# A decode step over two attention and MLP layers: ring of 3808 columns, three slots for the MLP weights of round one, two VectorE instructions fewer per head

## The chip, the cores and the metric

The kernel runs on one core of one Trainium2 chip. The metric is the device time of one execution in microseconds (us). The kernel before has a median of 712.35 us over three runs (711.5 to 712.86).

All data are float32. A column below means one float32 in each of 128 partitions, so 512 bytes; 512 columns are 0.262 MB.

## The reference, cut to what matters

Four sequences, one new token each, model width 640. A layer A (32 heads of width 128, the last 1024 positions of a cache) and a layer B (an MLP of width 1728 with relu) are applied twice, with the same weights and the same caches both times:

```
W = 1024; k = k_cache[:, :, -W:, :]; v = v_cache[:, :, -W:, :]      # B = 4, H = 32, Dh = 128

def A(x):
    q = (x @ wq) split into 32 heads
    p = softmax(einsum("bhqd,bhkd->bhqk", q, k) * Dh ** -0.5)
    return concat(einsum("bhqk,bhkd->bhqd", p, v)) @ wo

def B(x):
    return maximum(x @ w1, 0) @ w2

x = x + A(layernorm(x)); x = x + B(layernorm(x))      # round one
x = x + A(layernorm(x)); x = x + B(layernorm(x))      # round two
```

The four sequences have caches of their own, so each head needs its own 4 x 1024 keys and values, and each of them is used for one query only.

## The kernel before, in words

**Data in memory.** Each head has one record `rec` of `REC` = 9472 columns: 640 of wq (`WQ` to `K`), 4096 of keys (`K` to `V`), 4096 of values (`V` to `WO`), 640 of wo. Keys and values each come in two halves of `VH` = 2048 columns. The MLP weights `wm` are 17,280 columns: w1 as five blocks k of 1728, then w2 as 54 tiles of 160 (`W2` is the column where w2 begins, `WM` the end).

**Buffers in SBUF.** `store` holds five records (`NS` = 5) and, ahead of them, `FIRST` columns; `kept` holds the end of one record; `ring` has `RING` columns. The sum of `FIRST` and `RING` is the same before and after the change. In round one head 0 lies at the start of `store`, and its first `FIRST` columns stay there, so that round two need not load them again; the last five heads of round one (27 to 31) stay too, and round two begins with them (`order`). During the MLP of round one the five records therefore occupy `store`, and the weights pass through `ring` and through `spare`, 2560 columns (`PARKED`) in the middle of head 31's record. The data that lay there are moved to PSUM by four `park` copies (ScalarE) and brought back by `unpark` in round two.

**Order of the loads.** All loads are one list (`items`), issued in that order by SP (SyncE) on its one queue. `MLP_RING` cuts the weights of round one into pieces (from, to, buffer, column); after them `IN_RING` loads that part of head 0's record which isn't resident into `ring` and `spare`; after those, the heads 1 to 5 of round two go, in pieces, to places in the order in which they come free (`places`). A piece is issued when TensorE (PE) has read what stood in its place. So the places are slots: a piece that reuses the place of an earlier one waits until that one has landed, been multiplied and been released.

**One head.** `query` computes q; `scores` multiplies q with the keys, 128 columns of PSUM partitions being four groups of 32, one per sequence, of which only four rows were written; `softmax` is a maximum on VectorE (DVE) and an exponential on ScalarE (ACT), which also gives each partition's sum `tot`; `weights` transposes in 32x32 blocks and scales; `values`, `picks`, `output_T` and `project` finish the head. `scores` of the next head stands ahead of `values` of this one. In `weights` each of the four written rows of a group knows its own sum, and a transpose (`spread`) hands the sum to the other partitions.

**The MLP.** `mlp(0)` goes through w1 block by block (`h_ps`), then relu on DVE, then through w2 tile by tile (`acc`), in groups `W2_RING` after each of which `done` releases a piece. `busy` are matmuls whose result nobody reads; in `mlp(0)` one stands where a piece ends.

In the profile nearly every instruction has line L102, the line of the helper that records it, so groups are told apart by their tiles.

Of the kernel before, what the change touches and what calls it, by code (L numbers as in the profile page):

```python
# [34 lines left out]
OP = mybir.AluOpType  # L35
# [3 lines left out]
P = 128  # L39
B, D, H, DH, W, FF = 4, 640, 32, 128, 1024, 1728  # L40
# [6 lines left out]
WQ, K, V, WO = 0, D, D + 4 * W, D + 8 * W  # L47
REC = 2 * D + 8 * W
# [7 lines left out]
ENDS = 28  # L56
TILES[ENDS:ENDS] = [(13, 0), (13, 1)]
TCOLS = len(TILES) * FD
RING = 4320
KEPT = WO - 4 * 512  # L60
FIRST = K + 3 * 512
PARKED = 2560
FROM = V - 1024
W2 = KB * FF
WM = W2 + TCOLS


W2_RING = [8, 5, 16, 10, 11, 4]
MLP_RING = [(0, 1728, "ring", 0), (1728, 3456, "ring", 1728), (3456, 4320, "ring", 3456), (4320, 6480, "spare", 0),
            (6480, 8208, "ring", 0), (8208, W2 + 1280, "ring", 1728), (W2 + 1280, W2 + 2080, "ring", 3456),  # L70
            (W2 + 2080, W2 + 4640, "spare", 0), (W2 + 4640, W2 + 6240, "ring", 0), (W2 + 6240, W2 + 8000, "ring", 1600),
            (W2 + 8000, WM, "ring", 3456)]

IN_RING = [(2176, 4736, "spare", 0), (4736, 6272, "ring", 0), (6272, 8832, "ring", 1536)]

CUTS = [*range(0, K, DH), *range(K, WO, 512), *range(WO, REC + 1, FD)]
W1_SLOT = [[0, 1], [2, 3], [4]]
# [32 lines left out]
def decode_kernel(ctx: ExitStack, tc: tile.TileContext, xf, rec, wm, out):  # L110
    nc = tc.nc
    pe, dve, act, pool, sp = (InOrder(tc, e) for e in (nc.tensor, nc.vector, nc.scalar, nc.gpsimd, nc.sync))
# [5 lines left out]
    wT = scratch[:, :128].rearrange("p (i c j) -> p i c j", i=2, c=16)  # L118
# [4 lines left out]
    spread = scratch[:, 256:288]  # L123
    hT = scratch.rearrange("p (m j) -> p m j", j=32)
    oTs = sb.tile([P, LATE, B], F32, name="oTs")
    qT = sb.tile([P, B], F32, name="qT")
    of_batch = sb.tile([P, B], F32, name="of_batch")
# [3 lines left out]
    mrt = sb.tile([P, B], F32, name="mrt")  # L131
    small = sb.tile([P, 14], F32, name="small")
    nmax, rtot, rstd, eps, eps_dh, ones, unused, sums, tot0, tot1 = (small[:, i:i + 1] for i in range(10))
    squares = small[:, 10:]
    tot = [tot0, tot1]
    store = sb.tile([P, FIRST + NS * REC], F32, name="store")
    kept = sb.tile([P, REC - KEPT], F32, name="kept")
    ring = sb.tile([P, RING], F32, name="ring")

    sc_ps = [ps.tile([P, W], F32, name=f"sc_ps{i}") for i in range(2)]  # L140
# [39 lines left out]
    def home(h, r):  # L180

        if r:
            return FIRST + (h if h >= LAST else h - 6 + LAST) % NS * REC
        return (0 if h < NS else FIRST) + h % NS * REC

    items = []

    at = {("rec", 1, LAST - 1): [(KEPT, REC, "kept", 0)], ("rec", 1, 0): [(0, FIRST, "store", 0)]}
    live = []
    spare = home(H - 1, 0)  # L190
# [49 lines left out]
    ending(0, hs, True)  # L240
    for lo, hi, buf, col in MLP_RING:
        weight(0, lo, hi, buf, col)
# [3 lines left out]
    old = [home(h, 0) for h in hs[:NS]]  # L246
    new = hs[NS:]


    for lo, hi, buf, col in IN_RING:  # L250
        piece(1, new[0], lo, hi, *place(buf, col))
    places = [("store", old[i] + lo, old[j] + hi) for i, lo, j, hi in (
        (0, 0, 0, K), (0, K + 1024, 0, K + VH), (0, K + VH + 1536, 0, V), (1, 0, 1, K), (1, K, 1, K + VH), (1, K + VH, 1, V),
        (0, V, 0, WO), (2, 0, 2, V), (1, V, 1, REC), (3, 0, 3, V), (2, V, 2, REC), (3, V, 4, FROM))]
    places += [("store", 0, FIRST), ("store", old[4] + FROM, old[4] + REC), ("ring", 0, RING)]
    cuts = [h * REC + x for h in new[1:6] for x in CUTS]
    c, end = new[1] * REC, new[6] * REC
    for buf, lo, hi in places:
        if lo == old[1]:
            piece(1, new[0], WO, REC, buf, lo)  # L260
        elif c < end:
            cut = max(x for x in cuts if x <= min(end, c + hi - lo))
            run(1, c, cut, buf, lo)
            c = cut
# [36 lines left out]
    def done(key, lo, hi):  # L301
# [3 lines left out]
        if key == ("rec", 0, 0):  # L305
            lo = max(lo, FIRST)
        for x, y, buf, col in pieces(key):
# [91 lines left out]
    def scores(r, h, s, first=False):  # L399
        key = ("rec", r, h)  # L400
        for i in range(2):
            for b in range(B):
                pe.matmul(sc_ps[s][32 * b:32 * b + 4, 512 * i:512 * i + 512], qT[:, b:b + 1].to_broadcast([P, 4]),
                          cols(key, K + 512 * (B * i + b), 512), start=True, stop=True)
            done(key, K + VH * i, K + VH * i + VH)
            if first and i == 0:
                if r:
                    unpark(0)
                deviation(eps_dh, float(DH), True)
                act.activation(unused, eps, AF.Exp)  # L410
                if r:
                    unpark(1)
# [8 lines left out]

    def weights(s, parts=((0, 2),)):
        if parts[0][0] == 0:

            dve.transpose(spread, tot[s].to_broadcast([P, 32]))
            dve.reciprocal(rtot, spread[:, 0:1])
            dve.tensor_scalar(mrt, of_batch, rtot, None, op0=OP.mult)
        for i, j in parts:
            w = sc_ps[s][:, 512 * i:512 * j]
            dve.transpose(w, w)  # L430
            dve.tensor_tensor(wT[:, i:j].rearrange("p i c j -> p (i c) j"),
                              w.rearrange("p (c j) -> p c j", j=32)[:, :, :B],
                              mrt.unsqueeze(1).to_broadcast([P, 16 * (j - i), B]), op=OP.mult)

    def values(r, h, last=False, fill=(0, 0)):
        key = ("rec", r, h)
# [25 lines left out]
    def mlp(r):  # L462
# [21 lines left out]
        key = ("w", r)  # L484
        sizes = W2_SLOT if r else W2_RING
        first = 0
# [15 lines left out]
    for r in range(2):  # L502
# [12 lines left out]
        for n, h in enumerate(hs[:-2]):  # L515
            i = n - (H - late)
            s = (n + 1) % 2
# [87 lines left out]
```

## Time and profile before

| | |
|---|---|
| median of three runs | 712.35 us |
| profiled execution | 712.79 us, of which the span of instructions is 711.0 us |
| mean granted TensorE clock | 0.813 |
| busy: PE, DVE, ACT | 501.7 us (71%), 317.6 us (45%), 99.6 us (14%) |
| SP's load queue | 12528 packets, 301.42 MB, 98.9% of 16 engines' span |
| end of the loads | from 707 to 708 us the DMA engines are 1% busy; the store of the result follows |

How to read it: the share of the DMA engines and the moved GB/s by stretch tell where loads set the pace. PE's busy share is high because its clock is low in many stretches: in slices of 10 us it is granted between 0.50 and 1.00.

### The profile page before, as it was taken

Reading aid. Unit: us, or ns where it says so; the run is one execution under the profiler, and the core shown is the slowest. Engines: PE = TensorE matmul, PEld = TensorE weight load, DVE = VectorE, ACT = ScalarE, POOL = GpSimd, SP = SyncE. Lnnn points to the kernel's source line nnn. Section 1 sums busy time; section 2 is a strip of 40 time slices with the busy share of each in tenths; the row PEclk is TensorE's granted clock in tenths of the full one; section 3 lists DMA queues with packets and bytes.
Section 4 is the critical chain, followed back from the end, with each engine's and each line's share of the span. In section 5 each row is a group of like instructions: output and inputs, shape, how many; then the busy total and the mean of one; then the engine's idle time right before and its main releaser. Section 6 shows DMA issues by size and latency. Waiting matters only on the chain.

```text
span 711.0 us, 8606 instructions
## 1 busy us (share of the span) xinstructions
PE 501.7 (71%) x3722; PEld 203.5 (29%) x3722; DVE 317.6 (45%) x646; ACT 99.6 (14%) x210; POOL 1.1 (0%) x9
## 2 busy tenths in 40 slices
PE   0775684678584578869888999655584678686986
PEld 0331231232231223323223343222231232233322
DVE  3252362353353353545631876525162353454751
ACT  0110110011010110111120422101010011011120
POOL 0000000000000000000000000000000000000000
PEclk9987797677778776887999999859597677777999
DMA  9999999999999999999999999999999999999996
GB/s 397 435 417 450 425 431 443 421 439 439 424 435 441 427 436 419 424 438 426 429 398 403 402 427 436 442 438 436 435 420 444 431 435 430 429 433 419 429 427 281
DMA packets 12597, 301.97 MB, mean 425 GB/s; under 512 B 1408, under 2 KB 1552, under 8 KB 4624
## 3 DMA queue, kind: packets, MB, share of 16 engines
q1 hardware_dynamic: 12528, 301.42, 98.9%
q8 instruction: 29, 0.48, 0.2%
q14 instruction: 8, 0.07, 0.0%
q10 hardware_dynamic: 32, 0.01, 0.0%
HBM read 301.34 MB, written 0.08 MB: 424 GB/s over the span
## 4 chain that ended last, share of the span: by engine, by line
DMA 72%; PE 22%; DVE 4%; issue 1%; ACT 1%; ACTq 0%; SPq 0%; DVEq 0%
DMA store<-rec 65%; PE sc_ps L102 8%; PE o_ps L102 6%; DMA store<-wm 5%; PE acc L102 4%; PE misc L102 3%; DMA ring<-wm 2%; DVE scratch L102 1%; PE t_ps L102 1%; DVE o_ps L102 1%; ACT oTs L102 1%; DVE small L102 0%; DVE sc_ps L102 0%; ACT sc_ps L102 0%; ACTq L102 0%
## 5 line engine op out<-in xcount | busy, mean ns | idle before, releaser
L102 PE MATMUL sc_ps<-store,qT 128*4 128x512 f32 x1024 | 186.6, 821 | 42.4 <-DMA store<-rec 41.0
L102 PE MATMUL misc<-xT,store 128*128 128x4 f32 x620 | 95.7, 281 | 112.5 <-DMA store<-rec 112.5
L102 PE MATMUL o_ps<-store,scratch 128*16 128x512 f32 x960 | 145.8, 688 | 2.9 <-DVE scratch L102 1.8
L102 DVE TENSOR_REDUCE small<-sc_ps 128x1 f32<-128x1024 f32 x64 | 78.3, 1224 | 152.2 <-PE sc_ps L102 152.1
L102 PEld LDWEIGHTS misc<-xT,store 128*128 128x128 f32 x620 | 90.2, 227 | 169.9 <-DMA store<-rec 122.1
L102 ACT ACTIVATE sc_ps<-sc_ps,small 128x1024 f32<-128x1024 f32 x64 | 69.8, 1091 | 322.6 <-DVE small L102 322.6
L102 DVE STREAM_TRANSPOSE sc_ps<-sc_ps 128x1024 f32<-128x1024 f32 (+1 forms) x70 | 81.7, 1167 | 0.1
L102 PEld LDWEIGHTS sc_ps<-store,qT 128*4 128x4 f32 x1024 | 31.8, 104 | 121.6 <-issue 62.7
L102 PEld LDWEIGHTS o_ps<-store,scratch 128*16 128x16 f32 x960 | 33.1, 114 | 114.8 <-issue 96.7
L102 DVE TENSOR_TENSOR o_ps<-o_ps,of_block 128x512 f32<-128x512 f32 x62 | 43.3, 699 | 48.3 <-PE o_ps L102 48.1
L102 DVE TENSOR_TENSOR qT<-misc,rows 128x4 f32<-128x4 f32 x61 | 9.5, 155 | 115.7 <-PE misc L102 115.7
L102 PE MATMUL acc<-store,oTs 128*4 128x160 f32 x488 | 33.8, 361 | 17.0 <-ACT oTs L102 17.0
L102 DVE TENSOR_REDUCE scratch<-o_ps 128x128 f32<-128x512 f32 x62 | 42.9, 691 | 2.1
L102 ACT COPY oTs<-t_ps 128x4 f32<-128x4 f32 x59 | 9.6, 162 | 206.6 <-PE t_ps L102 206.6
L102 PE MATMUL t_ps<-rows,scratch 128*128 128x4 f32 x118 | 25.3, 285 | 11.3 <-DVE scratch L102 10.3
L102 PEld LDWEIGHTS t_ps<-rows,scratch 128*128 128x128 f32 x118 | 21.3, 225 | 16.9 <-DVE scratch L102 13.7
L102 DVE TENSOR_TENSOR scratch<-sc_ps,mrt 128x128 f32<-128x128 f32 (+1 forms) x70 | 19.6, 280 | 2.9 <-PE o_ps L102 0.3
L102 PE MATMUL acc<-kept,small 128*1 128x328 f32 (+2 forms) x54 | 18.0, 440 | 0.0
L102 DVE TENSOR_SCALAR mrt<-of_batch,small 128x4 f32<-128x4 f32 x64 | 14.7, 229 | 2.2
L102 DVE STREAM_TRANSPOSE scratch<-small 128x32 f32<-128x32 f32 x64 | 12.9, 201 | 2.4 <-ACT sc_ps L102 2.4
L102 PEld LDWEIGHTS acc<-store,oTs 128*4 128x4 f32 x488 | 7.2, 86 | 22.7 <-ACT oTs L102 22.1
L102 ACT ACTIVATION_READ_ACCUMULATOR sc_ps<-sc_ps,small 128x1 f32 x64 | 12.3, 193 | 0.0
(85 smaller groups left out, 116.3 us busy)
## 6 DMA issues: line engine op xcount, KB each, us to landing
store<-rec SPq DMA_DIRECT2D x14, 7872.0 KB, 27.4
store<-rec SPq DMA_DIRECT2D x7, 7936.0 KB, 30.3
store<-rec SPq DMA_DIRECT2D x4, 7104.0 KB, 30.9
store<-rec SPq DMA_DIRECT2D x11, 2368.0 KB, 36.1
store<-rec SPq DMA_DIRECT2D x3, 4736.0 KB, 25.7
store<-rec SPq DMA_DIRECT2D x2, 4416.0 KB, 29.0
store<-rec SPq DMA_DIRECT2D x3, 2048.0 KB, 40.2
store<-rec SPq DMA_DIRECT2D x1, 4160.0 KB, 21.4
```

The source lines that it names most:

```text
L102: r = build(*args, **kwargs)
```

## The change

It does four things.

1. `RING` falls from 4320 to 3808 columns, and `FIRST` rises from 2176 to 2688: 512 columns more of head 0's record stay, and `IN_RING` loads 6144 columns instead of 6656.
2. The MLP weights of round one come in nine pieces instead of eleven. They used four slots (three in `ring`, one in `spare`); now they use three (two in `ring`, one in `spare`). `W2_RING` follows.
3. Head 0's rest goes to other places (`ring`, `ring`, `spare` instead of `spare`, `ring`, `ring`), and in `places` the ring stands ahead of the last piece of `store`.
4. `scores` writes all 32 rows of a group instead of four (`to_broadcast([P, 32])`). So every partition has its own sum, and `weights` drops the transpose into `spread` and the multiplication into `mrt`; the tensor_tensor that scaled by `mrt` becomes a scalar_tensor_tensor which multiplies by `rtot` and by `of_batch`.

```diff
-RING = 4320
+RING = 3808
 KEPT = WO - 4 * 512
-FIRST = K + 3 * 512
+FIRST = K + 4 * 512
...
-W2_RING = [8, 5, 16, 10, 11, 4]
-MLP_RING = [(0, 1728, "ring", 0), (1728, 3456, "ring", 1728), (3456, 4320, "ring", 3456), (4320, 6480, "spare", 0),
...
+W2_RING = [4, 16, 10, 13, 11]
+MLP_RING = [(0, 1728, "ring", 0), (1728, 3456, "ring", 1792), (3456, 5616, "spare", 0), (5616, 7344, "ring", 0),
...
-IN_RING = [(2176, 4736, "spare", 0), (4736, 6272, "ring", 0), (6272, 8832, "ring", 1536)]
+IN_RING = [(2688, 4224, "ring", 0), (4224, 6272, "ring", 1664), (6272, 8832, "spare", 0)]
...
-    places += [("store", 0, FIRST), ("store", old[4] + FROM, old[4] + REC), ("ring", 0, RING)]
+    places += [("store", 0, FIRST), ("ring", 0, RING), ("store", old[4] + FROM, old[4] + REC)]
...
-                pe.matmul(sc_ps[s][32 * b:32 * b + 4, 512 * i:512 * i + 512], qT[:, b:b + 1].to_broadcast([P, 4]),
+                pe.matmul(sc_ps[s][32 * b:32 * b + 32, 512 * i:512 * i + 512], qT[:, b:b + 1].to_broadcast([P, 32]),
                           cols(key, K + 512 * (B * i + b), 512), start=True, stop=True)
...
-            dve.transpose(spread, tot[s].to_broadcast([P, 32]))
-            dve.reciprocal(rtot, spread[:, 0:1])
-            dve.tensor_scalar(mrt, of_batch, rtot, None, op0=OP.mult)
+            dve.reciprocal(rtot, tot[s])
...
-            dve.tensor_tensor(wT[:, i:j].rearrange("p i c j -> p (i c) j"),
-                              w.rearrange("p (c j) -> p c j", j=32)[:, :, :B],
-                              mrt.unsqueeze(1).to_broadcast([P, 16 * (j - i), B]), op=OP.mult)
+            dve.scalar_tensor_tensor(wT[:, i:j].rearrange("p i c j -> p (i c) j"),
+                                     w.rearrange("p (c j) -> p c j", j=32)[:, :, :B], rtot,
+                                     of_batch.unsqueeze(1).to_broadcast([P, 16 * (j - i), B]), op0=OP.mult,
+                                     op1=OP.mult)
```

SP's queue between the two rounds. `ring<-wm` and `store<-wm` are pieces of the MLP weights (`store` here is the slot `spare`), `ring<-rec` and the next `store<-rec` are the rest of head 0; behind the name stands partitions x columns. Before:

```order
L102 DMA ring<-wm 128x1728 x2
L102 DMA ring<-wm 128x864
L102 DMA store<-wm 128x2160
L102 DMA ring<-wm 128x1728
L102 DMA ring<-wm 128x1712
L102 DMA ring<-wm 128x800
L102 DMA store<-wm 128x2560
L102 DMA ring<-wm 128x1600
L102 DMA ring<-wm 128x1760
L102 DMA ring<-wm 128x640
```

And now:

```order
L101 DMA ring<-wm 128x1728 x2
L101 DMA store<-wm 128x2160
L101 DMA ring<-wm 128x1728
L101 DMA ring<-wm 128x1936
L101 DMA store<-wm 128x2560
L101 DMA ring<-wm 128x1600
L101 DMA ring<-wm 128x2080
L101 DMA store<-wm 128x1760
L101 DMA ring<-rec 128x1536
L101 DMA ring<-rec 128x2048
```

The three small pieces of 864, 800 and 640 columns are gone; two pieces (3456 columns) instead of three (4320) stand in the queue ahead of the first that needs `spare`, and the last piece of the weights has 1760 columns instead of 640.

VectorE in one head of the steady part, from the maximum over one head's scores to the last instruction of the same `weights`. `small` holds the maximum, the sums and `rtot`; `sc_ps_74` the scores; `scratch` the transposed weights. Before:

```order
L102 TENSOR_REDUCE small<-sc_ps_74 128x1
L102 TENSOR_TENSOR o_ps<-o_ps,of_block 128x512
L102 TENSOR_REDUCE scratch<-o_ps 128x128
L102 TENSOR_TENSOR qT<-misc,rows 128x4
L102 STREAM_TRANSPOSE scratch<-small 128x32
L102 RECIPROCAL small<-scratch 128x1
L102 TENSOR_SCALAR mrt<-of_batch,small 128x4
L102 STREAM_TRANSPOSE sc_ps_74<-sc_ps_74 128x1024
L102 TENSOR_TENSOR scratch<-sc_ps_74,mrt 128x128
```

And now:

```order
L101 TENSOR_REDUCE small<-sc_ps_74 128x1
L101 TENSOR_TENSOR o_ps<-o_ps,of_block 128x512
L101 TENSOR_REDUCE scratch<-o_ps 128x128
L101 TENSOR_TENSOR qT<-misc,rows 128x4
L101 RECIPROCAL small<-small 128x1
L101 STREAM_TRANSPOSE sc_ps_74<-sc_ps_74 128x1024
L101 SCALAR_TENSOR_TENSOR scratch<-sc_ps_74,small,of_batch 128x128
```

The transpose of the sums and the multiplication into `mrt` are gone, and the scaling has three operands; the rest keeps its order.

TensorE from the end of w1's fifth block to the end of w2 follows the pieces. Before, from the relu on:

```order
L102 MATMUL acc<-ring,scratch 4x160 x8
L102 MATMUL acc<-kept,small 1x328
L102 MATMUL acc<-ring,scratch 4x160 x5
L102 MATMUL acc<-kept,small 1x328
L102 MATMUL acc<-store,scratch 4x160 x17
L102 MATMUL acc<-kept,small 1x328
L102 MATMUL acc<-ring,scratch 4x160 x11
L102 MATMUL acc<-kept,small 1x328
L102 MATMUL acc<-ring,scratch 4x160 x15
```

And now:

```order
L101 MATMUL acc<-ring,scratch 4x160 x4
L101 MATMUL acc<-kept,small 1x328
L101 MATMUL acc<-store,scratch 4x160 x16
L101 MATMUL acc<-kept,small 1x328
L101 MATMUL acc<-ring,scratch 4x160 x12
L101 MATMUL acc<-kept,small 1x328
L101 MATMUL acc<-ring,scratch 4x160 x13
L101 MATMUL acc<-store,scratch 4x160 x11
```

The matmuls `acc<-kept,small` are `busy`; one less stands among the tiles of w2 (and one less among the blocks of w1), and behind the landing of the last piece come 11 tiles; before, the last two pieces held 11 and 4, one group of 15. (Two tiles of w2 take two matmuls each, hence 17 and 12.)

More of the change, by code (lines that the diff above doesn't have):

```diff
@@ L65 @@
 WM = W2 + TCOLS
-W2_RING = [8, 5, 16, 10, 11, 4]
-MLP_RING = [(0, 1728, "ring", 0), (1728, 3456, "ring", 1728), (3456, 4320, "ring", 3456), (4320, 6480, "spare", 0),
-            (6480, 8208, "ring", 0), (8208, W2 + 1280, "ring", 1728), (W2 + 1280, W2 + 2080, "ring", 3456),
-            (W2 + 2080, W2 + 4640, "spare", 0), (W2 + 4640, W2 + 6240, "ring", 0), (W2 + 6240, W2 + 8000, "ring", 1600),
-            (W2 + 8000, WM, "ring", 3456)]
-IN_RING = [(2176, 4736, "spare", 0), (4736, 6272, "ring", 0), (6272, 8832, "ring", 1536)]
+W2_RING = [4, 16, 10, 13, 11]
+MLP_RING = [(0, 1728, "ring", 0), (1728, 3456, "ring", 1792), (3456, 5616, "spare", 0), (5616, 7344, "ring", 0),
+            (7344, W2 + 640, "ring", 1792), (W2 + 640, W2 + 3200, "spare", 0), (W2 + 3200, W2 + 4800, "ring", 0),
+            (W2 + 4800, W2 + 6880, "ring", 1664), (W2 + 6880, WM, "spare", 0)]
+IN_RING = [(2688, 4224, "ring", 0), (4224, 6272, "ring", 1664), (6272, 8832, "spare", 0)]
 CUTS = [*range(0, K, DH), *range(K, WO, 512), *range(WO, REC + 1, FD)]
```

## The prediction

> **What bounds the kernel now.** First the page: span, busy shares, the 40 slices, the load queue, the chain that ended last by engine.
>
> ```profile
> span 711.0 us, 8606 instructions
> PE 501.7 (71%) x3722; PEld 203.5 (29%) x3722; DVE 317.6 (45%) x646; ACT 99.6 (14%) x210; POOL 1.1 (0%) x9
> DMA  9999999999999999999999999999999999999996
> DMA packets 12597, 301.97 MB, mean 425 GB/s; under 512 B 1408, under 2 KB 1552, under 8 KB 4624
> q1 hardware_dynamic: 12528, 301.42, 98.9%
> DMA 72%; PE 22%; DVE 4%; issue 1%; ACT 1%; ACTq 0%; SPq 0%; DVEq 0%
> ```
>
> The 16 DMA engines are busy in every slice but the last; 301.42 MB took 98.9% of 711.0 us, so the loads set the pace at 301.42 / 703.2 = 0.4286 MB/us. The chain names DMA for 72% and PE for 22%, but that PE time lies beside loads that were running anyway. So I read the windows by stretch (us, length, PE busy (count), granted clock, DMA share, GB/s).
>
> ```profile
> 0.00:345.00 345.00, 232.33 (x1550) 0.79 1.00 430
> 345.00:360.00 15.00, 9.72 (x74) 1.00 0.99 417
> 360.00:400.00 40.00, 34.66 (x341) 0.96 0.99 398
> 400.00:454.00 54.00, 49.30 (x432) 0.94 1.02 434
> 454.00:700.00 246.00, 171.14 (x1234) 0.78 1.00 431
> 700.00:711.00 11.00, 4.58 (x112) 1.00 0.46 189
> ```
>
> Nothing but bytes counts in the long stretches: share 1.00, 430 and 431 GB/s. From 360 to 400 us, the MLP of round one and the start of round two, the share is still 0.99 but the rate 398: 15.9 MB, which at 430 would take 37.0 us. So 40 - 37.0 = 3.0 us are all that the junction can give back, and the part of the change that can cost time lies there too. Windows of 2 us show where the queue runs thin:
>
> ```profile
> 368.00:370.00 2.00, 1.00 0.90 341
> 370.00:372.00 2.00, 1.00 1.01 402
> 372.00:374.00 2.00, 1.00 0.89 350
> 392.00:394.00 2.00, 1.00 0.96 377
> 396.00:398.00 2.00, 1.00 0.95 370
> ```
>
> At 368 and 372 about a tenth of 2 us is empty, 0.2 us each; between 392 and 398 it is 0.1 us twice. The issues of SP (start, us, what, count) say why:
>
> ```profile
> 354.81 5.89 SPq L102 DMA_DIRECT2D ring<-wm  x3
> 363.74 0.33 SPq L102 DMA_DIRECT2D store<-wm  x1
> 368.04 0.33 SPq L102 DMA_DIRECT2D ring<-wm  x1
> 373.87 0.33 SPq L102 DMA_DIRECT2D store<-wm  x1
> ```
>
> The third piece of `ring` (864 columns) is in the queue before 363.74, when the last `park` lets the piece in `spare` go; the next can go only at 368.04, when PE has done w1's first block. By then the queue is nearly used up.
>
> **The change part by part.**
>
> *Bytes.* 512 columns less, 0.262 MB, at 0.4286 MB/us: -0.61 us, certain as far as the loads set the pace. Of this the Trainium skill (DMA: Bandwidth & Descriptors, Specifications) has another price: it limits a core's HBM reads to about 358 GB/s, by which the 0.262 MB would be worth 0.73 us, by its figure an estimate; the trace, with 430 GB/s over 345 us, is above that limit, so the trace's rate is used.
>
> *Two pieces fewer.* What a packet costs beside its bytes comes from two stretches of the load queue (packets, MB, share), the first from 270 to 345 us with large pieces, the second from 372 to 400 us with small ones:
>
> ```profile
> q1 hardware_dynamic: 1328, 32.05, 99.2%
> q1 hardware_dynamic: 2090, 11.04, 98.4%
> ```
>
> 75 us x 16 x 0.992 = 1190.4 engine-us = 1328 a + 32.05 c, and 28 x 16 x 0.984 = 440.8 = 2090 a + 11.04 c give a = 18.9 ns per packet. A piece has 128 packets, one per partition, and 16 short ones (1408 under 512 B on the page, for 87 loads and stores), so two pieces are 288 x 18.9 ns / 16 = 0.34 us. The second stretch holds stalls of the thin queue as well, so 18.9 ns is an upper end and 0 the lower; I take -0.2 us.
>
> *Three slots for four.* The 864 columns that stood ahead of the 2160 are 0.442 MB, 1.03 us of queue, which is missing from 363.74 on. Issues after PE's first block (368.04) are not earlier, since that block starts on pieces already there. If all 16 engines ran dry together at 368, the 1.03 us would be lost whole; if the cover is still enough, nothing; and if the larger pieces close both thin spots, 0.4 us is gained. The engines don't run dry together, as 341 GB/s over 2 us (and not 0) shows: a part of them had work. I take 0.4, nearer to the thin spots' 0.2 each than to 1.03. Later reissues follow a landed piece, as before; the three remaining slots hold 6368 columns, 7.6 us of queue, against 8.2.
>
> *End of the MLP.* PE's last tiles before (start, us, what):
>
> ```profile
> 385.67 1.26 PE acc L102 x30
> ```
>
> 15 tiles (30 records) in 1.26 us are 0.084 us per tile; they end at 386.9. They began with the landing of the piece of 11 tiles, and the 4 tiles that landed behind it were covered. Now 11 tiles (0.92 us) follow the very last landing: where that comes at the same time as before, at some 386 us, PE ends up to 0.6 us later, and 0 at best. I take 0.3. One `busy` less among the tiles stands ahead of waits for data and buys nothing. What round two releases (from 389 us on) comes later by that, and the spots at 392 and 396 show that the loads wait for just these releases; the DMA engines also get there 0.4 us earlier, with less to do. So there up to 0.7 us is empty in place of the 0.2. I take +0.3.
>
> *VectorE.* The removed rows, their neighbours and the new form on small tiles (busy us, mean ns | idle before):
>
> ```profile
> L102 DVE STREAM_TRANSPOSE scratch<-small 128x32 f32<-128x32 f32 x64 | 12.9, 201 | 2.4 <-ACT sc_ps L102 2.4
> L102 DVE TENSOR_SCALAR mrt<-of_batch,small 128x4 f32<-128x4 f32 x64 | 14.7, 229 | 2.2
> L102 DVE TENSOR_TENSOR scratch<-sc_ps,mrt 128x128 f32<-128x128 f32 x58 | 16.9, 291 | 2.0
> L102 DVE SCALAR_TENSOR_TENSOR xT<-sc_ps,xT 128x20 f32<-128x20 f32 x4 | 0.7, 178 | 1.2 <-PE sc_ps L102 1.2
> L102 DVE TENSOR_TENSOR scratch<-xT 128x20 f32<-128x20 f32 x4 | 0.7, 179 | 0.1
> ```
>
> 64 x (201 + 229) ns = 27.5 us of DVE work go. The three-operand form costs the same at 128x20 (178 against 179 ns); at 128x128 I take 291 ns again, between that and double. It is hidden by the loads: DVE is busy 45%. On a chain that frees buffers it stands once, in round two's first head (start, us, what):
>
> ```profile
> 394.90 0.22 DVE scratch L102
> 395.15 0.17 DVE small L102
> 395.35 0.23 DVE mrt L102
> 396.52 2.08 PE o_ps L102 x16
> ```
>
> Some 0.45 us earlier, so PE's `values` and all that it releases until 454 us. That pays back the +0.3 for releases after 398 us, not for those at 392 to 396, which `scores` gives. Further on the queue is long: 1.3 MB for the ring landed 23.8 us after issue,
>
> ```profile
> ring<-rec SPq DMA_DIRECT2D x1, 1344.0 KB, 23.8
> ```
>
> of which its bytes are 3.2 us. So nothing more is gained, and the late part of `places`, whose cuts move too, has 20 us of cover. Cover gone, these 54 us (PE 49.30 busy) would be bound by PE, and the 0.45 us would show.
>
> *32 rows for four.* Loads of 4, 16 and 128 columns of weights, and matmuls that write 4 and 16 rows:
>
> ```profile
> L102 PEld LDWEIGHTS sc_ps<-store,qT 128*4 128x4 f32 x1024 | 31.8, 104 | 121.6 <-issue 62.7
> L102 PEld LDWEIGHTS o_ps<-store,scratch 128*16 128x16 f32 x960 | 33.1, 114 | 114.8 <-issue 96.7
> L102 PEld LDWEIGHTS misc<-xT,store 128*128 128x128 f32 x620 | 90.2, 227 | 169.9 <-DMA store<-rec 122.1
> 407.76 1.72 PE sc_ps L102 x16
> 409.47 1.72 PE o_ps L102 x16
> ```
>
> At one clock 4 and 16 rows take the same 1.72 us, so 32 should. The load lies between 114 and 227 ns, nearest to 16 columns: I take 125, beside running matmuls; exposed, 20 ns per head, covered by loads. Price 0, at worst below.
>
> *Sum.* -0.61 - 0.2 + 0.4 + 0.3 = -0.1 us. The profiled execution took 712.79, 1.8 outside its span, and lies 0.44 above the median of 712.35; from the median the forecast is 712.2. Ends: -0.61 - 0.34 - 0.4 + 0 = -1.35, and -0.61 - 0 + 1.03 + 0.7 = +1.1.
>
> **Rivals.** A, *slower: the three slots run dry at each turn*. A slot's turn is landing, PE's block, issue, first bytes; the other two slots must cover it. Two slots are some 4300 columns, 5.1 us at 0.4286, but the engines' stagger eats into it. For: the queue ran thin twice even with four slots. Against: between the two thin windows the share is back at 1.01, and each loses only 0.2 us. If each of seven reissues loses 0.35 us, that is 2.5 - 0.8 = +1.7: 714.0. It decides once all losses exceed 0.8 + 1.4 = 2.2 us.
>
> B, *faster: larger pieces heal the junction*. Half of the 3.0 us comes back, if stalls and not bytes made 398 GB/s: -0.61 - 1.5 = -2.1, 710.2. For: the low rate has the small pieces. Against: the 864 columns ahead of `spare` were cover, not ballast.
>
> C, *each piece pays a fixed time of its own*. The store of the result landed 1.6 us after issue (KB, us),
>
> ```profile
> out<-scratch SPq DMA_DIRECT2D x1, 80.0 KB, 1.6
> ```
>
> 0.2 of it bytes. Two such 1.4 us and the bytes: -3.4, 708.9. Against: a share of 0.89 and more in the thin stretch leaves no such holes. The Trainium skill (DMA: Bandwidth & Descriptors, Anatomy of one DMA) fits about 2.0 us fixed per DMA on the GpSimd path, by which two fewer would be worth 4.0 us and the time 707.7, an estimate; the shares speak against both.
>
> D, *slower: weight loads of 32 columns at the price of 128*, not hidden: 123 ns x 16 x 10 heads is 20 us of PE from 391 to 454, more than the queue's lead; the loads would stop some us: 715. Against: matmuls run beside them.
>
> E, *the bytes saved are waited away* at 392 us entirely: 712.4, no change.
>
> **How the numbers follow.** 0.2% of 712.35 is 1.4 us, about what a measurement of this kernel can tell from no change (the three runs span 1.36). Forecast 0.67 and E 0.08 end within; A 0.10 and D 0.01 are slower; B 0.13 and C 0.01 faster. So faster 0.14, same 0.75, slower 0.11. The likeliest one's own range is 711.0 to 713.4; to keep the other cases to 2 in 10 I go to 710.4 and 713.8, which also holds the spread of a median of runs.
>
> **What would show it.** Bytes: 301.16 MB on the load queue and 288 packets fewer. Slots: DMA share near 0.8 in the 2 us after PE's first block, and thinner at 392. Junction: the stretch 360 to 400 moves 0.26 MB less in about the same time. VectorE: 518 instructions, some 27 us less busy. 32 rows: `scores` still 1.72 us per head between 400 and 430. I am wrong if the rate of the junction leaves 390 to 410, or if PE's clock or the matmuls with 32 rows change so that the loads wait outside it.

## The result, and the profile after

The changed kernel takes 716.96 us (median of nine runs, 714.08 to 719.28), the kernel before, run beside it, 712.23 us (nine runs, 710.74 to 713.78). The ratio is 1.0058, 95% interval 1.0041 to 1.0075: slower by 3 to 5 us. The forecast was no change, 712.2 us, and its range ended at 713.8. The runs also lie further apart than before, over 5 us instead of 3.

The profiled execution of the changed kernel took 714.56 us, 2.4 us less than the median, so the profile can't show the whole loss. From its page, the span, the busy shares, the packets and the load queue:

```profile
span 712.7 us, 8468 instructions
PE 498.9 (70%) x3718; PEld 210.7 (30%) x3718; DVE 293.1 (41%) x518; ACT 99.6 (14%) x210; POOL 1.1 (0%) x9
q1 hardware_dynamic: 12240, 301.16, 98.8%
```

Fewer bytes, fewer packets, less VectorE, and yet a longer span. The windows by stretch (us, length, PE busy (count), granted clock, DMA share, GB/s) say where:

```profile
0.00:345.00 345.00, 225.19 (x1550) 0.80 1.00 430
360.00:400.00 40.00, 32.79 (x322) 0.91 0.97 363
400.00:454.00 54.00, 49.96 (x434) 0.94 1.02 435
454.00:700.00 246.00, 175.78 (x1242) 0.76 1.00 431
```

All stretches but one read as before (430, 434, 431 GB/s there). From 360 to 400 us the rate is 363 GB/s instead of 398: 14.5 MB instead of 15.9, so 1.4 MB are late, 3.3 us at 0.4286 MB/us, of which the saved bytes give 0.6 back. The span of this execution is only 1.7 us longer than before (712.7 against 711.0), so 1.0 of these 2.7 us is made good behind 400 us: the load queue moves 0.17 MB more than before from 400 to 700 us, which is 0.4 us, and the rest comes back after that. The chain of the junction, its longer pieces (start, us, what):

```profile
364.27 7.03 DMA store<-wm
...
371.35 1.63 PE sc_ps L101 x10
...
373.00 7.60 DMA store<-wm
...
380.64 1.81 PE acc L101 x23
...
382.47 6.09 DMA store<-wm
...
388.60 0.86 PE acc L101 x19
...
394.66 1.22 DVE small L101
```

This is the slot `spare`, used three times running: issued, landed, multiplied, released, and issued again 0.02 us later. It has no slack: a piece takes 6.1 to 7.6 us from issue to landing, and PE 1.6 to 1.8 us to release it. The first maximum of round two starts at 394.66. In the chain of the kernel before, with two pieces as long, it started at 392.04:

```profile
369.61 6.73 DMA ring<-wm
...
378.79 6.84 DMA ring<-wm
...
392.04 1.23 DVE small L102
```

The waits of PE between 364 and 396 us (engine and tile, what it waited for: us in total, times, longest), first of the changed kernel, then of the kernel before:

```profile
PE acc L101 <- DMA store<-wm: 3.5, 2, 1.8
PE sc_ps L101 <- DMA ring<-wm: 1.4, 2, 0.9
PE sc_ps L101 <- DMA store<-wm: 1.1, 1, 1.1
```

```profile
PE acc L102 <- DMA ring<-wm: 1.8, 2, 1.3
PE sc_ps L102 <- DMA ring<-wm: 1.1, 2, 0.6
PE sc_ps L102 <- DMA store<-wm: 0.9, 1, 0.9
```

PE waits 6.0 us for pieces instead of 3.8, while the DMA engines wait for PE. The windows of 2 us show both sides:

```profile
368.00:370.00 2.00, 2.00 (x14) 1.00 0.88 307
372.00:374.00 2.00, 1.51 (x8) 1.00 0.85 303
378.00:380.00 2.00, 0.97 (x10) 1.00 0.88 340
380.00:382.00 2.00, 1.36 (x24) 0.63 1.04 346
382.00:384.00 2.00, 2.00 (x28) 0.51 0.96 384
```

The rate is thin at 368, 372 and 378, behind each wave of reissues, not only at the first; and from 380 to 384 the granted clock drops to 0.63 and 0.51 after PE was busy for only 0.97 of 2 us. Before, it was 1.00 there:

```profile
380.00:382.00 2.00, 1.87 (x38) 1.00 0.99 379
```

The DMA share hardly tells of the loss: over the 40 us it falls from 0.99 to 0.97, and the rate from 398 to 363 GB/s.

### The profile page after: what moved, and what is told of

It reads as the page before. It is cut to its first block, busy times and chain, and to the rows that moved or that the text cites. A ratio compares the mean times of both kernels' runs of the same rounds, so it can differ in the third digit from the quotient of the medians.

```text
span 712.7 us, 8468 instructions
## 1 busy us (share of the span) xinstructions
PE 498.9 (70%) x3718; PEld 210.7 (30%) x3718; DVE 293.1 (41%) x518; ACT 99.6 (14%) x210; POOL 1.1 (0%) x9
## 3 DMA queue, kind: packets, MB, share of 16 engines
q1 hardware_dynamic: 12240, 301.16, 98.8%
## 4 chain that ended last, share of the span: by engine, by line
DMA 72%; PE 22%; DVE 4%; ACT 1%; issue 1%; ACTq 0%; SPq 0%; DVEq 0%
DMA store<-rec 65%; PE sc_ps L101 8%; DMA store<-wm 7%; PE o_ps L101 6%; PE misc L101 3%; PE acc L101 3%; DVE scratch L101 2%; PE t_ps L101 1%; DVE o_ps L101 1%; ACT oTs L101 1%; DVE small L101 0%; DVE sc_ps L101 0%; ACT sc_ps L101 0%; ACT o_ps L101 0%; ACTq L101 0%
## 5 line engine op out<-in xcount | busy, mean ns | idle before, releaser
L101 PE MATMUL sc_ps<-store,qT 128*32 128x512 f32 x1004 | 183.8, 821 | 37.6 <-DMA store<-rec 36.2
L101 PEld LDWEIGHTS sc_ps<-store,qT 128*32 128x32 f32 x1004 | 40.3, 139 | 109.2 <-issue 57.0
L101 DVE SCALAR_TENSOR_TENSOR scratch<-sc_ps,small,of_batch 128x128 f32<-128x128 f32 (+1 forms) x70 | 23.7, 339 | 2.7
L101 PE MATMUL acc<-store,scratch 128*4 128x160 f32 x166 | 7.8, 331 | 7.7 <-DMA store<-wm 7.7
L101 DVE RECIPROCAL small<-small 128x1 f32<-128x1 f32 x64 | 9.8, 153 | 2.3 <-ACT sc_ps L101 2.3
```

Source lines behind the costliest of these rows:

```text
L101: r = build(*args, **kwargs)
```

## The experiments

Ratios are to the kernel before, run beside each on the same chip, with 95% intervals; times are medians. The letters of theories are those of each expectation. "Junction" is the stretch 360 to 400 us, and its rate is that of one profiled execution.

**Part 4 alone and the ring part alone.** First the kernel before with the new `scores` and `weights`:

```diff
-                pe.matmul(sc_ps[s][32 * b:32 * b + 4, ...], qT[:, b:b + 1].to_broadcast([P, 4]), ...
+                pe.matmul(sc_ps[s][32 * b:32 * b + 32, ...], qT[:, b:b + 1].to_broadcast([P, 32]), ...
...
-            dve.transpose(spread, tot[s].to_broadcast([P, 32]))
...
-            dve.tensor_scalar(mrt, of_batch, rtot, None, op0=OP.mult)
...
```

> The kernel before with part 4 of the change alone (32 rows in scores, three-operand scaling); ring, pieces and bytes as before. Theory S (three slots starve the loads at the junction, the head part is free): 711.8 to 712.8 us, ratio 0.999 to 1.001, the stretch 360 to 400 us at 395 to 400 GB/s. Rival H (the 32 rows disturb TensorE's clock or its pace, and that starves the loads): 715 to 717 us and under 380 GB/s in that stretch.

711.62 us against 711.92, ratio 0.9996 (0.9987 to 1.0006); the junction as before:

```profile
360.00:400.00 40.00, 35.27 (x342) 0.96 1.01 398
```

Then the changed kernel with these lines put back as before:

> The changed kernel with scores and weights as before, so parts 1 to 3 alone. Theory S: as slow as the whole change, 715 to 718 us, with runs spread over some 5 us; 355 to 370 GB/s from 360 to 400 us. Rival H: 711.5 to 712.2 us, the bytes saved and nothing lost.

715.01 us, ratio 1.0053 (1.0033 to 1.0072):

```profile
360.00:400.00 40.00, 30.86 (x318) 0.96 0.95 362
```

The loss is whole without part 4, and part 4 alone moves nothing that its interval of 0.1% would show. That is theory S.

**Nine pieces in the ring of before.** `RING`, `FIRST`, the heads and the order of `places` of before, with the nine pieces in three slots:

```diff
-W2_RING = [8, 5, 16, 10, 11, 4]
+W2_RING = [4, 16, 10, 13, 11]
... (MLP_RING of the changed kernel)
-IN_RING = [(2176, 4736, "spare", 0), (4736, 6272, "ring", 0), (6272, 8832, "ring", 1536)]
+IN_RING = [(2176, 3712, "ring", 0), (3712, 6272, "ring", 1664), (6272, 8832, "spare", 0)]
```

> The kernel before with its ring of 4320 columns, its 2176 resident columns and its heads, but the weights of round one in the nine pieces of the changed kernel (three slots, 3456 columns ahead of the piece that waits for the last park). Theory S: slow too, and 0.6 us slower than the ring part alone since no bytes are saved: 715.5 to 718.5 us. Rival R (not the slots but the smaller ring or the other places of head 0's rest cost the time): 712 to 713 us.

715.01 us, ratio 1.0056 (1.0037 to 1.0076), so rival R falls:

```profile
360.00:400.00 40.00, 29.48 (x318) 1.00 0.97 364
```

So it isn't the smaller `RING`, nor the 512 columns that stay, nor the order of `places`: the cut of the weights, together with where head 0's rest goes, makes the loss.

**Four small slots in the ring of 3808.** The changed kernel with twelve pieces:

```diff
-W2_RING = [4, 16, 10, 13, 11]
-MLP_RING = [(0, 1728, "ring", 0), (1728, 3456, "ring", 1792), (3456, 5616, "spare", 0), ...
+W2_RING = [4, 16, 8, 8, 7, 11]
+MLP_RING = [(0, 1296, "ring", 0), (1296, 2592, "ring", 1296), (2592, 3456, "ring", 2592), (3456, 5616, "spare", 0), ...
```

> The changed kernel, ring of 3808 columns, but the ring cut into three slots of 1296, 1296 and some 1200 columns, so four slots with spare and twelve pieces; the columns ahead of the piece that waits for the last park stay 3456. Theory S1 (what counts is how many slots turn over, since a smaller slot is released sooner): 711 to 713 us, the stretch 360 to 400 at 395 GB/s or more. Theory S2 (what counts is the depth of the queue in columns, above all the 864 columns missing ahead of the park): no better than the change, 715 to 718 us, and thin at 366 to 372.

714.11 us, ratio 1.0042 (1.0022 to 1.0062). Theory S1 falls, and the time is below the 715 to 718 of S2: a fourth slot, with the columns left as few, gives little back. In each turn its pieces hold as many columns as those of the changed kernel: 5616, 6224 and 5440. Two of the twelve executions took 719.8 us, the profiled one among them. Its timeline and windows show what such an execution has (start, us, what, and in brackets PE's wait ahead of it; then the windows as above):

```profile
388.62 0.86 PE L102 MATMUL acc<-store,scratch 128*4 128x160 f32 x19 [1.71 <-DMA store<-wm]
```

```profile
390.00:392.00 2.00, 1.96 (x10) 0.58 0.99 404
392.00:394.00 2.00, 2.00 (x12) 0.50 0.99 393
394.00:396.00 2.00, 2.00 (x10) 0.50 0.87 338
396.00:398.00 2.00, 2.00 (x13) 0.71 0.73 180
```

The last landing comes at the same time as in the profile of the changed kernel, after a wait as long:

```profile
388.60 0.86 PE L101 MATMUL acc<-store,scratch 128*4 128x160 f32 x19 [1.78 <-DMA store<-wm]
```

But here the clock then falls to 0.50, round two's first head runs at half pace, its releases come late, and the loads drop to 180 GB/s at 396. So the loss seems to have a second stage, which strikes in some executions only.

**The cover ahead of `spare`.** The kernel before, with the piece of 864 columns issued behind the piece of `spare` instead of ahead of it:

```diff
-(1728, 3456, "ring", 1728), (3456, 4320, "ring", 3456), (4320, 6480, "spare", 0),
+(1728, 3456, "ring", 1728), (3456, 5616, "spare", 0), (5616, 6480, "ring", 3456),
```

> The kernel before, all its slots, pieces sizes and bytes, but the 864-column piece stands behind the 2160-column piece of spare in the queue, so 3456 columns instead of 4320 are ahead of the piece that waits for the last park. Theory C (the missing cover before the park starts the loss): 712.8 to 714 us, under 385 GB/s from 360 to 400. Theory L (the loss is made at the end of the weights, where the last piece has to wait for spare): 711.6 to 712.4 us.

713.0 us, ratio 1.0011 (1.0000 to 1.0022), junction 387 GB/s: theory C's time, though not its rate of under 385. This is the loss that the prediction had taken at 0.4 us and at most at 1.03; by the ratio it is 0.8, and anything from 0 to 1.6 by the interval. The other way round, the changed kernel with its third piece split, so that its first part waits for less of the park (it was issued at 360.93 instead of 364.27 us):

```diff
-(3456, 5616, "spare", 0),
+(3456, 5184, "spare", 0), (5184, 5616, "spare", 2048),
```

> The changed kernel, with the third piece of the weights split: 1728 columns at the start of spare, whose place the third park frees some 3 us before the last, and 432 behind it. Everything later as in the changed kernel. Theory C: 711.5 to 712.5 us, and no thin window at 364 to 372 us. Theory L: unchanged, 714 to 717 us.

715.21 us, ratio 1.0056 (1.0037 to 1.0075), junction 370 GB/s, as theory L had it. From 364 to 366 us the rate is back at 416 GB/s, but from 366 to 370 it stays thin (366 and 292 GB/s). So this mends the first thin spot in part only, and the time shows nothing of it.

**The last piece.** The kernel before with its last 1760 columns through `spare` at the end of the list:

```diff
-W2_RING = [8, 5, 16, 10, 11, 4]
+W2_RING = [8, 5, 16, 10, 4, 11]
...
-            (W2 + 2080, W2 + 4640, "spare", 0), (W2 + 4640, W2 + 6240, "ring", 0), (W2 + 6240, W2 + 8000, "ring", 1600),
-            (W2 + 8000, WM, "ring", 3456)]
+            (W2 + 2080, W2 + 4640, "spare", 0), (W2 + 4640, W2 + 6240, "ring", 0), (W2 + 6240, W2 + 6880, "ring", 3456),
+            (W2 + 6880, WM, "spare", 0)]
```

> The kernel before, with 4320 columns ahead of the park and eleven pieces, but at the end 640 columns go to the ring and the last 1760 of the weights to spare, behind the piece of 2560; head 0's rest follows in ring, ring, spare. Theory L: 713.5 to 715 us, the first product of round two 1.5 to 2.5 us later than before (392.0 there is the start of the first maximum). Theory C: 711.6 to 712.4 us.

719.56 us, ratio 1.0106 (1.0082 to 1.0130), junction 356 GB/s: above both ranges, and worse than the whole change. The edit does more than send the last piece through `spare`. The middle of `ring`, where 1712 columns of the weights stood, isn't loaded again until head 0's rest, and that stands in the queue behind the last piece. So for one turn this kernel, too, holds fewer columns. The timeline and the windows again:

```profile
388.36 0.86 PE L102 MATMUL acc<-store,scratch 128*4 128x160 f32 x19 [3.78 <-DMA store<-wm]
```

```profile
382.00:384.00 2.00, 1.92 (x38) 1.00 0.71 175
...
386.00:388.00 2.00, 0.00 (x0) 1.00 1.04 333
...
390.00:392.00 2.00, 2.00 (x10) 0.50 1.03 394
392.00:394.00 2.00, 2.00 (x12) 0.50 0.98 343
394.00:396.00 2.00, 2.00 (x14) 0.50 0.85 289
```

PE has nothing at all to do from 386 to 388, and from 390 on it runs at 0.50. To tell the late piece from the clock, the same kernel with ten filler matmuls (`busy`) ahead of the last piece:

```diff
-            if r == 0 and i < len(sizes) - 2:
-                busy()
+            if r == 0:
+                for _ in range((1, 1, 1, 1, 10, 0)[i]):
+                    busy()
```

> The kernel of the seventh experiment (last 1760 columns through spare, 719.6 us) with ten filler matmuls more in front of the last piece, where TensorE waited 3.8 us and fell to half its clock afterwards. Theory K (about half of that loss is the clock, in the first head of round two): granted clock 1.00 from 388 to 398 us, 714 to 716 us. Rival: the loads alone are late, the clock only fills time that was lost anyway: 718 to 720 us.

716.04 us, ratio 1.0054 (1.0041 to 1.0066), junction 366 GB/s:

```profile
388.00:390.00 2.00, 2.00 (x28) 1.00 1.02 425
390.00:392.00 2.00, 2.00 (x16) 1.00 1.00 346
392.00:394.00 2.00, 2.00 (x18) 1.00 0.90 348
```

The clock stays at 1.00, and the time is at the edge of theory K's range. Without fillers the loss was 7.6 us (719.56 against 711.93), with them it is 4.3 (716.04 against 711.69). So by the medians ten matmuls whose result nobody reads are worth 3.3 us here (the two profiled executions, 717.47 and 716.26, lie 1.2 us apart), and the clock is what their traces show to differ behind the wait. The other 4.3 are the late piece, the place left empty and what waits for them.

**Mending the changed kernel.** More fillers, the counts behind the groups of w2 being 4, 1, 1, 5, 0 instead of one behind each of the first three (eight more, where the expectation counts seven):

> The changed kernel with seven more filler matmuls (busy) in round one's w2: three more behind its first group of tiles, five behind its fourth, where TensorE waits for a piece, and none taken away but one. Theory K (a part of the loss, and the runs near 718 to 720 us, come from TensorE's clock falling to half while it waits for pieces): 713 to 714.5 us, without runs above 716, and a granted clock of 1.00 from 364 to 400. Rival: the clock only follows, and the time stays at 714 to 717 us with runs up to 720.

715.14 us, ratio 1.0041 (1.0028 to 1.0055):

```profile
360.00:400.00 40.00, 34.91 (x342) 1.00 0.97 368
```

In the profiled execution (713.77 us, the lowest of eight) the clock is 1.00 throughout, and the highest of the eight is 716.5 instead of 719.3 us. But 1.004 stays, above the 713 to 714.5 us of theory K. Then the piece of 2560 columns in two:

```diff
-(W2 + 640, W2 + 3200, "spare", 0)
+(W2 + 640, W2 + 2400, "spare", 0), (W2 + 2400, W2 + 3200, "spare", 1760)
```

> The changed kernel, its ring, resident columns and three slots, but the 2560-column piece of w2 in spare comes as 1760 and 800 columns, so that the last 1760 of the weights wait only for the first of them. Theory L (what costs the time is that the last piece of the weights is issued late and lands alone): issued 1.5 us earlier, PE goes into round two 1 to 2 us earlier than in the changed kernel, 712 to 713.5 us, most runs under 715. Rival T (the loss is spread over the whole junction, since three slots hold fewer columns in flight): 714 to 716 us, as the changed kernel.

715.41 us over five executions (a sixth, of 1174.64 us, is left out), ratio 1.0053 (1.0034 to 1.0072), junction 364 GB/s. The last piece was issued 1.3 us earlier (381.13 instead of 382.47 us), and nothing came of it: rival T, not theory L. All of these mends together, with the first 512 columns of head 0's rest in `spare` and ten fillers instead of three:

> The changed kernel with the split of the 2560 columns, the split of the first spare piece (1728 and 432), the first 512 columns of head 0's rest in spare ahead of the ring, and five more filler matmuls. If L and K hold: 711 to 712.5 us, no run above 714. If T holds: 713 to 714.5 us.

714.22 us, ratio 1.0038 (1.0026 to 1.0051), clock 1.00, junction 373 GB/s. That is T's range; mends of single places leave most of the loss.

**Columns or slots.** The remaining four change the number of columns that the slots hold together, the number of slots, or both. Three slots with the 6880 columns of before, in the kernel before, with fillers (3, 2, 3, 0, so eight):

```diff
+W2_RING = [13, 16, 13, 12]
+MLP_RING = [(0, 2160, "ring", 0), (2160, 4320, "ring", 2160), (4320, 6480, "spare", 0), (6480, W2, "ring", 0),
+            (W2, W2 + 2080, "ring", 2160), (W2 + 2080, W2 + 4640, "spare", 0), (W2 + 4640, W2 + 6720, "ring", 0),
+            (W2 + 6720, WM, "ring", 2160)]
```

> The kernel before, its ring of 4320, resident columns and heads, but the MLP weights of round one in eight pieces: three slots of 2160, 2160 and 2560 columns, 6880 in all as before, instead of 6300 in the kernel with nine pieces; seven fillers behind its groups of w2. Theory T (the rate at the junction is the columns in the slots over the time of a turn, some 8.9 us in both traces; the number of slots does not matter): 6880 x 512 B / 8.9 us = 396 GB/s from 360 to 400, 711.5 to 713 us. Rival N (three slots are too few, or larger pieces are released too late): 360 to 375 GB/s, 714 to 717 us.

714.34 us, ratio 1.0032 (1.0021 to 1.0043), at 380 GB/s: neither the 396 of theory T nor the 360 to 375 of rival N. The same with some 7300 columns, new heads and fillers (`RING` 4832, `FIRST` 1664, so 0.262 MB more to load):

```diff
+MLP_RING = [(0, 2160, "ring", 0), (2160, 4752, "ring", 2160), (4752, 6912, "spare", 0), (6912, W2 + 320, "ring", 0), ...
```

> The step the other way, as a candidate for a faster kernel: ring of 4832 columns, 1664 resident ones (512 less than before, so 0.61 us more bytes), three slots of 2160, 2592 and 2560 columns (7300 in use), the new scores and weights, nine fillers. Theory T: 7300 x 512 B / 8.9 us = 420 GB/s at the junction, 2 us won there, 0.6 paid: 709.5 to 711.5 us. Rival N or a turn that grows with the pieces: 712.5 to 715 us.

713.46 us, ratio 1.0024 (1.0012 to 1.0036), at 388 GB/s instead of theory T's 420: the rival's range. As many columns in four slots, with the new heads and one filler behind each of the first three groups:

```diff
+MLP_RING = [(0, 1728, "ring", 0), (1728, 3456, "ring", 1728), (3456, 4752, "ring", 3456), (4752, 6912, "spare", 0), ...
```

> The kernel before with its four slots, but with 512 columns more in the ring and 512 fewer of head 0 resident (so 0.262 MB more to load, +0.61 us at the trace's 0.4286 MB/us), ten pieces instead of eleven, and the new heads, which the run of part 4 alone showed to be free. The slots hold some 7300 columns instead of 6880. Theory T, the columns in the slots set the rate of the junction (rate = columns x 512 B / a turn of 8.85 us): 7300 columns give up to 422 GB/s between 360 and 400 us instead of 398, 2.3 us less, against 0.6 us more bytes: ratio 0.996 to 0.999, 709.5 to 711.5. Theory S, the cut sets it (three slots or four, and how large the piece is that must be multiplied whole before its place comes free), columns beyond that nothing: with four slots and pieces as large as before the rate stays at 395 to 400 and only the bytes are paid: ratio 1.000 to 1.002. If even four slots with more columns fall below 390 GB/s, neither is right and the place of each reissue in TensorE's work decides.

713.03 us against 712.88, ratio 1.0007 (0.9992 to 1.0022), at 401 GB/s: theory S's time, and not T's gain. The junctions of the three, in this order:

```profile
360.00:400.00 40.00, 33.14 (x334) 1.00 0.98 380
```

```profile
360.00:400.00 40.00, 34.55 (x343) 1.00 0.97 388
```

```profile
360.00:400.00 40.00, 33.98 (x346) 1.00 1.00 401
```

And the four small slots with the clock held up by fillers (3, 3, 2, 2, 3, 0):

> The kernel with four small slots again (about 6270 columns, twelve pieces), with more filler matmuls behind the groups of w2 (3, 3, 2, 2, 3, 0 instead of one each), so that TensorE's granted clock should stay at 1.00 from 360 to 400 us, where it fell to 0.50 in the profile of the run without them. Theory V, cover: what counts is what the other slots hold while one slot turns (columns of all slots less one slot on average). That is 4700 columns here, 4245 in the changed kernel (363 GB/s between 360 and 400 us), 4590 in three big slots (380), 4870 in three bigger ones (388), 5160 before (398), 5480 with four bigger ones (401). So 381 to 386 GB/s are expected, and with 0.61 us of bytes saved a ratio of 1.001 to 1.003. Theory T, columns in the slots in all over a turn of 8.9 us: 361 GB/s, a ratio of 1.004 to 1.006. If the clock falls nonetheless, the run tells nothing on either.

714.63 us, ratio 1.0046 (1.0032 to 1.0060). Its windows, and the longest piece of PE in its chain:

```profile
360.00:400.00 40.00, 37.61 (x346) 0.96 0.95 366
380.00:390.00 10.00, 10.00 (x129) 1.00 0.89 335
```

```profile
378.12 11.14 PE acc L102 x131
```

This run doesn't decide. The rate, 366, is near the 361 of the columns and not the 381 to 386 of the rule of cover; but PE is now busy for all of 380 to 390, and its work stands in the chain as one piece of 11.14 us, with the fillers of the last groups in it. Thirteen fillers, meant to hold the clock up, lengthened the path themselves.

Taken together:

| columns in the slots | three slots | four slots |
|---|---|---|
| about 6300 | 363 (changed), 364 GB/s; 1.0058, 1.0056 | 347 (clock 0.50), 366 (fillers); 1.0042, 1.0046 |
| 6880 | 380; 1.0032 | 398 (before); 1 |
| about 7300, 0.61 us more bytes | 388; 1.0024 | 401; 1.0007 |

The seventh experiment, the kernel before with its last piece in `spare`, stands outside the table. It has four slots and 6880 columns, and still 356 GB/s (366 with fillers), since one place is empty for a turn.

At three slots more columns raise the rate: 363 (368 with fillers), 380, 388 GB/s. At 6880 columns four slots move 18 GB/s more than three, and the time is 0.3% less; at about 6300 columns the fourth slot shows no gain beyond the intervals. At four slots 6880 columns are enough: 432 more give 3 GB/s, 0.12 MB over the junction and less than half of the 0.262 MB that they cost. My reading is that the loads need room for everything that is on its way or being multiplied during a turn of some 9 us. A slot that is freed in one stroke adds to the turn: in the kernel with three slots and 6880 columns the first piece, 2160 columns, reaches into w1's second block, and its reissue came at 369.51 us instead of 368.04.

## Why the prediction was wrong

**The mechanism was in it, as rival A at 0.10; the step that failed is "three slots for four", taken at +0.4 us (ends -0.4 and +1.03).** It counted the cover once, at 363.74 us, and set the later turns to nothing: "Later reissues follow a landed piece, as before." The run of the cover alone agrees with that price (1.0011, about 0.8 us). In place of 0.4 us the junction of the profiled execution lost 3.3 us, and the kernel before with nothing changed but the nine pieces in three slots, and head 0's rest behind them, is at 1.0056. The windows at 372 and 378 us and the chain through `spare` show that the later turns lost too. The sum wrote down the number that matters, "6368 columns, 7.6 us of queue, against 8.2", and didn't hold it against the length of a turn, which the trace of before had: `spare` was issued at 363.74, 373.87 and 382.04 us, 9.15 us a turn on average. In the changed kernel the issues are at 364.27, 373.00 and 382.47 us, 9.1 a turn. So the turn stayed as long, the room fell by 7%, and the rate fell by 9%. Had the forecast scaled the rate with the room, 398 x 6368 / 6880 = 368 GB/s, it would have had a loss of 40 x (398 - 368) = 1.2 MB, 2.8 us, less 0.6 us of bytes. This is worked out after the result, and it isn't a law (see what stays open).

**The thin spots were sized by the wrong column.** "0.2 us each" comes from the DMA share, 0.90 and 0.89 of 2 us. By the rates in the same lines, 341 and 350 of 430 GB/s, each lost 0.4 us. The 0.4 of the sum and rival A's 0.35 a reissue both lean on the smaller size.

**Rival A's own price was too small too.** 0.35 us at each of seven reissues gave 714.0. With more fillers, the clock at 1.00 in the execution that was profiled, the changed kernel stays at 1.0041, 2.9 us. With the 0.8 us of savings that the forecast counted this is 3.7 us lost, 0.5 us at each if it is spread over the seven.

**The clock was left out of the sum.** It stood only among what would make the forecast wrong. The median of the changed kernel is 1.0058, with fillers 1.0041: some 1.2 us, though the intervals overlap. That it can be worth microseconds is shown on the kernel with the late last piece (3.3 us by the medians); that it makes the longer executions of the changed kernel itself is inferred, since the one profile of that kernel is of an execution of 714.56 us.

**"End of the MLP", +0.3 us, was too small.** The landing of the last piece was put "at some 386 us", as before; its matmuls began at 388.60, and the first maximum of round two came 2.6 us later than before. The 11 tiles behind the landing were right (0.86 us here, 0.92 estimated); the landing was late, by the turns ahead of it.

**Bytes and pieces.** 301.16 MB and 288 packets fewer, as forecast. That two pieces fewer are worth 0.2 us can't be seen beside the loss.

**VectorE was free, and the estimate of its instruction was low.** There are 518 instructions, and 24.5 us less busy instead of 27.5. The three-operand form at 128x128 takes 350 ns, not 291:

```profile
L101 DVE SCALAR_TENSOR_TENSOR scratch<-sc_ps,small,of_batch 128x128 f32<-128x128 f32 x58 | 20.3, 350 | 2.0
```

The cover named, the loads, held: the run of part 4 alone is at 0.9996.

**32 rows were free.** The weight load of 32 columns takes 139 ns (125 estimated), and `scores` 1.72 us per head as before:

```profile
L101 PEld LDWEIGHTS sc_ps<-store,qT 128*32 128x32 f32 x1004 | 40.3, 139 | 109.2 <-issue 57.0
```

```profile
403.68 1.72 PE sc_ps L101 x16
```

**Rival B, larger pieces heal the junction, fell:** the junction got worse. **Rivals C and D fell:** no gain of microseconds from two pieces fewer, no loss from the weight loads. E fell with the time. Of the signs that the forecast named, the thin 2 us after PE's first block came, if less thin than its 0.8 (0.88 at 368, and 0.85 at 372), and the rate of the junction left 390 to 410, which was its own condition for being wrong.

**What stays open.** That the cut into three slots makes the loss is shown; which of its properties does is not. The runs don't separate what a slot more is worth from what smaller pieces are worth, nor from where the last piece goes: sent through `spare` in the kernel before, it cost 4.3 us with the clock up, but it left a place empty there, and the two kernels with three larger slots, whose last piece goes to `ring`, still lose 1.0032 and 1.0024. The law by which columns and slots act together isn't settled either. Columns over a turn of 8.9 us would give 396 and 420 GB/s for the two kernels with three larger slots, where 380 and 388 were measured, and 420 for the larger one with four, where it was 401. The turn isn't fixed: between the issues of `spare` it is 9.7, 10.9 and 9.9 us in these three, and 8.7, 9.6 and 9.0 us in the profiles of the ring part alone, of the nine pieces in the ring of before and of the changed kernel with fillers. And the room isn't what is in use: the pieces of the changed kernel fill 5616, 6224 and 5440 of its 6368 columns in three turns, those of before 6480, 6800 and 6560 of 6880. No version beat the kernel before; part 4 alone equals it.

## What to carry to other kernels

Where loads go through slots that are freed by work on the loaded data, hold the columns of all slots against the whole turn, from issue over landing and multiplying to the next issue: if the stretch already moves no more than the columns per turn, expect a column taken away to cost at every turn, not once. Count the columns that the pieces fill, and read what a thin stretch lost from its GB/s, since the DMA share hardly fell here. Look at the chain: a slot that stands in it three times running, each time issued as soon as it is released, has no slack. And count what the waits do to TensorE's clock: ten fillers ahead of a wait of 3.8 us were worth 3.3 us here, but fillers on the path are work like any other.

## What the runs showed of the hardware

At the junction PE's granted clock fell to 0.50 after PE had been idle for a part of the time, not in step with how long one wait was. A wait of 3.78 us was followed by 0.50 from 390 to 396 us. Waits of 1.71 and 1.78 us at the same place were followed by 0.50 in one kernel and by 1.00 in the other:

```profile
390.00:392.00 2.00, 1.97 (x15) 1.00 1.00 373
```

The Trainium skill (TensorE: Matmul & The Clock Gate, What's actually happening) says that the clock halves after an idle window of some 3.4 us, and that the window runs freely instead of starting with the work. The lengths agree with such a window. Cut at the edges of the fall, the changed kernel has 0.50 for 3.41 us:

```profile
377.12:380.53 3.41, 1.36 (x15) 1.00 1.02 364
380.53:383.94 3.41, 3.30 (x44) 0.50 0.97 351
```

The kernel with four small slots and the one with the late last piece have it for 6.83 us, twice as long (390.33 to 397.16 and 389.86 to 396.69 us). But the window ahead of a fall wasn't idle: PE was busy for 1.36 of 3.41 us here, and for 1.66 and 1.45 us in those two. Around its wait of 1.78 us the changed kernel has 2.12 us on the same grid, and no fall. So where a wait lies in the window seems to decide, and a window less than about half busy seems to be enough. The runs don't set a threshold: two windows with 1.55 and 1.56 us on these grids weren't followed by a fall (383.03 to 386.45 us with the late last piece, 373.26 to 376.68 us with four small slots).

What the slowed matmuls release comes late: from 394 to 402 us the kernel with the late last piece moves 218 to 289 GB/s, and the same kernel with fillers 300 to 390.
